# Blocks 0 and 1 of the first layer take turns, and eight attention steps form the start

## The chip, the cores and the metric

The kernel runs on one core of a Trainium2 chip. The engines that matter are TensorE (PE in the profile; its weight loads are PEld), VectorE (DVE), ScalarE (ACT), GpSimd (POOL), and SyncE (SP), which here issues DMAs. The metric is the device time of one execution in microseconds; less is better.

## What is computed

Attention over chunks of 32 queries with 8 memory keys, then two dense layers, each up, activation, down. Cut to what matters:

```
q, k, v: (4, 8, 768, 64)    mem_k, mem_v: (4, 8, 8, 64)
for each chunk c of 32 queries:
    k_full = concat(mem_k, k[c*32-16 : c*32+40]);  v_full likewise
    a = softmax(q_c @ k_full.T / 8);               out_c = a @ v_full
x = out as 3072 tokens x 512
h = x @ w_in1;  x = (h * sigmoid(1.702 * h)) @ w_out1     # 512 -> 2048 -> 512
h = x @ w_in2;  x = (max(h,0) + alpha * min(h,0)) @ w_out2
```

## The kernel before

**Tiling.** The 3072 tokens are cut into six blocks of 512, the 2048 hidden units into 16 chunks of 128. A *step* is one block and one chunk f: `mm1` makes the hidden tile h (12 matmuls of 128x512, L312), the activation and `split_g` make from it a high part gh and a low part gl (ACT and DVE), and `mm2_t` adds the chunk's share to four PSUM banks y0 to y3 (12 matmuls, L342). Every product is made of three matmuls, high x high, high x low and low x high, so a step has 24. Layer 1 has 96 steps, layer 2 another 96. mm2 trails mm1 by one step (`LAG`). After a block's last chunk `finish1` scales the four banks and stores them to the DRAM tensor y1, from which layer 2 reads.

**Weights.** Chunk f of a layer is loaded by `w_load` (two DMAs of 512 KB, L85 and L89), then prepared by `w_abs` (ACT, L96), `w_bits` (four DVE instructions on 128x1024, L102 to L109), `w_high` (ACT, L120) and `w_low` (DVE, L125). `w_tick` does one such chunk and loads ahead. Layer 1 prepares its 16 chunks while block 0 runs through all of them; later blocks find them ready in SBUF.

**Attention.** 24 *attention steps* of 128 tokens give the input x of the blocks, four steps to a block. A step loads q, k and v (512, 416 and 416 KB), makes scores (32 small PE instructions in the profile, L195), maximum, difference and exponential (DVE, DVE, ACT), sum and scaling (DVE, L227 to L232), transposes in two groups (PE, L242), copies them (ACT, L247), multiplies with v (L256), and writes the high part of x by ACT (L270) and the low part by DVE (L271). An mm1 of a block reads all 512 tokens, so it needs all four steps.

**Order.** Steps 0 to 3 run ahead of the main loop (L425 on) in a pool with two places for loads (`SB = 2`). Then the main loop goes through the steps, block by block, and `attend` spreads the later attention steps evenly: steps 4 to 7 during block 0, and so on. A scheduler turns this into one fixed order for each engine. Each engine and each DMA queue works through its own order; an instruction whose input is missing holds all behind it. All loads and stores stand in SP's queue.

Of the kernel before, what the change touches and what calls it, by code (L numbers as in the profile page):

```python
# [31 lines left out]
P2_BLOCKS = [512] * 6  # L32
TBM = 512
LAG = 1
NSTART = 4
WTICKS = (2, 3)
WAHEAD = 2
LEAD = 4
OPB = 3
W0 = 3  # L40
WN = 5
# [8 lines left out]
def fused_kernel(ctx: ExitStack, tc: tile.TileContext, qs, ks, vs, ident, w_in1, w_out1, w_in2, w_out2, alpha, out):  # L50
    nc = tc.nc
    PSUM = bass.MemoryType.PSUM
    const = ctx.enter_context(tc.tile_pool(name="const", bufs=1))
# [76 lines left out]
    def w_tick(limit):  # L130
        s = wtick[0]
        if s >= limit + 1:
            return False
        if s - 1 in wst:
            w_low(s - 1)
        while wloaded[0] < limit and wloaded[0] <= s + (WAHEAD if wloaded[0] < BOOST else 1):
# [20 lines left out]
    run = [slice(0, KW), slice(NK - KW, NK)]  # L157
    half = [slice(0, 64), slice(64, 128)]

    def att_open(name, bufs, nq):  # L160
        ap["pb"] = 2 * bufs if bufs > 1 else 1
# [13 lines left out]
        return (ps2 if tag == "h" else ps1).tile(shape, F32, tag=tag, name=name)  # L175

    def a_load(m):
        q = ap["pool"].tile([128, 2, HP, 2, 64], F32, tag="q", name=f"q{m}")
        nc.sync.dma_start(out=q.rearrange("p g j c q -> p (g j c q)"), in_=qs[m])
        k = ap["pool"].tile([128, 2, HP, NK], F32, tag="k", name=f"k{m}")  # L180
        nc.sync.dma_start(out=k.rearrange("p g j n -> p (g j n)"), in_=ks[m])
        st[m] = dict(q=q, k=k)

    def a_load_v(m):
        t = ap["pool"].tile([NK, 2, VC], F32, tag="v", name=f"v{m}")
        nc.sync.dma_start(out=t, in_=vs[m])
        st[m]["v"] = t

# [34 lines left out]
    def a_norm(m):  # L223
        s = st[m]
        ex = s["ex"]
        sm = ap["pool"].tile([128, 2 * HP], F32, tag="sm", name=f"sm{m}")
        nc.vector.tensor_reduce(out=sm, in_=ex, axis=mybir.AxisListType.X, op=ALU.add)  # L227
        nc.vector.tensor_scalar(out=sm, in0=sm, scalar1=1e-9, scalar2=None, op0=ALU.add)
        nc.vector.reciprocal(sm, sm)
        pr = ap["pr"][m % len(ap["pr"])]  # L230
        for c in range(2):
            nc.vector.tensor_tensor(  # L232
                out=pr[half[c], :, :, run[c]].rearrange("p g j n -> p (g j) n"), in0=ex[half[c]],
                in1=sm[half[c]].rearrange("p (g n) -> p g n", n=1).to_broadcast([64, 2 * HP, KW]), op=ALU.mult,
            )
        s["pr"] = pr

    def a_trans(m, g, tag=None):
        s = st[m]
        s["pt", g] = bank([NK, HP, 128], tag or f"a{g}", f"pt{m}_{g}")  # L240
        for j in range(HP):
            nc.tensor.transpose(s["pt", g][:, j, :], s["pr"][:, g, j, :], id_sb)  # L242

    def a_pcopy(m, g):
        s = st[m]
        s["p", g] = ap["pool"].tile([NK, HP, 128], F32, tag=f"p{g}", name=f"p{m}_{g}", bufs=ap["pb"] if g == 0 else None)
        nc.scalar.copy(s["p", g], s["pt", g])  # L247

    def a_pv(m, tag="a0"):
# [87 lines left out]
    def mm2_t(p, y, gs, n, f):  # L337
        gh, gl = gs
        wh, wl = wt[p, f]
        for m in range(NKC):  # L340
            for i, (w, g) in enumerate(((wh, gh), (wh, gl), (wl, gh))):
                nc.tensor.matmul(  # L342
                    y[m][:, :n], w[:, 1, m * 128:(m + 1) * 128], g[:, :n],
                    start=(f == 0 and i == 0), stop=(f == NF - 1 and i == 2),
                )

    def mm2_n(p, y, gs, n, f):
# [6 lines left out]
                    start=(f == 0 and i == 0), stop=(f == NF - 1 and i == 2),  # L354
                )

    def finish1(y, t0, n):
        for m in range(NKC):
            o = op.tile([128, TBM], F32, tag="o", name="o")
            if m % 2:  # L360
# [30 lines left out]
    steps = []  # L391
    t0 = 0
    for j, n in enumerate(P1_BLOCKS):
        steps += [(1, j, t0, n, f) for f in range(NF)]
        t0 += n
    t0 = 0
    for j, n in enumerate(P2_BLOCKS):
        steps += [(2, j, t0, n, f) for f in range(NF)]
        t0 += n
    n1 = len(P1_BLOCKS)  # L400
    need = [done_tick(int(p1_start[j + 1]) // SQ - 1) for j in range(n1)]
    last1 = (n1 - 1) * NF

    pend = {}
    ys = {}
# [5 lines left out]
    for i in range(NWARM):  # L411
        nc.tensor.matmul(t, warm, warm, start=True, stop=True)

    att_open("as", SB, 2)
    a_load(0)
    a_load_v(0)
    w_load(0)
    nc.sync.dma_start(out=id_sb, in_=ident)
    a_load(1)
    wloaded[0] = 1  # L420
    stags = ("a0", "a1", "y2", "y3")
# [3 lines left out]
    for t in range(NSTART + 1):  # L425
        if t + 1 < NSTART:
            a_scores(t + 1, stags[(t + 1) % 4])
            a_load_v(t + 1)
        if t + 2 < NSTART:
            a_load(t + 2)  # L430
        if t < NSTART:
            a_norm(t)
            for g in range(2):
                a_trans(t, g, "h")
                a_pcopy(t, g)
        if t + 1 < NSTART:
# [12 lines left out]
    att_open("at", 1, 1)
    a_load(NSTART)  # L450
    a_load_v(NSTART)

    def do_mm2(i):
        p, j, t0, n, f = steps[i]
        if f == 0:
            ys[p, j] = [ps1.tile([128, DM], F32, tag=f"y{m}", name=f"y{m}") for m in range(NKC if p == 1 else n // 128)]
        (mm2_t if p == 1 else mm2_n)(p, ys[p, j], pend.pop(i), n, f)
        if f == NF - 1:
            (finish1 if p == 1 else finish2)(ys.pop((p, j)), t0, n)

    def attend(j, h):
        goal = need[j] + (need[j + 1] - need[j]) * min(1, h / (2 * NF - LEAD))
        while tick[0] < goal:
            a_tick()

    for i, (p, j, t0, n, f) in enumerate(steps):
        if i < NF:
            while wtick[0] < min(NPC + 1, W0 + (WN * f) // 4):
                w_tick(NPC)
        if i == last1:  # L470
# [71 lines left out]
```

## Time and profile before

| | us |
|---|---|
| median of 3 runs (1182.45 to 1184.22) | 1183.54 |
| the profiled execution | 1184.33 |
| its span, first to last instruction | 1182.6 |
| PE busy, share of span | 1150.4, 97% |
| DVE busy | 611.1, 52% |
| ACT busy | 321.5, 27% |

[...] The timeline lists instructions with the idle time before each and what ended it, in brackets. Matmuls overlap in the records (one of 128x512 lasts 0.39 us, the next starts 0.23 us later), so that their pace is read from runs of many, not from one.

### The profile page before, as it was taken

The numbers are of one execution on the slowest core, as the hardware profiler recorded it, in microseconds if no ns is written. First come the engines' busy times: TensorE is split into PE (matmuls) and PEld (weight loads), VectorE is DVE, ScalarE is ACT, GpSimd is POOL, SyncE is SP. The second block draws the span as 40 slices with busy tenths as digits, with TensorE's granted clock in tenths as the row PEclk, the third lists the DMA queues.
The fourth block names the chain that finished last, engine by engine and source line by source line (L and its number), as shares of the span: only waits on it lengthen the run. The fifth ranks groups of instructions, "written<-read, shape, count | busy, mean of one in ns | idle before, by whom it ended". The sixth has DMA issues, their size and how long they took to land.

```text
span 1182.6 us, 14925 instructions
## 1 busy us (share of the span) xinstructions
PE 1150.4 (97%) x6364; PEld 942.3 (80%) x6364; DVE 611.1 (52%) x871; ACT 321.5 (27%) x479; POOL 2.4 (0%) x10
## 2 busy tenths in 40 slices
PE   5799999999999999999999999999999999999998
PEld 5577788888888888888888788888888888888886
DVE  5899934343343434343699874434434434344433
ACT  2555433232323223223456321111111111111111
POOL 0000000000000000000000000000000000000000
PEclk8799999999999999999999999999999999999999
DMA  6964313121121212112544500200100000000000
GB/s 211 275 220 155 133 69 94 47 75 55 50 91 60 70 48 83 48 62 71 191 166 145 189 23 1 72 1 5 67 1 1 36 1 1 36 1 8 29 1 36
DMA packets 43578, 86.49 MB, mean 73 GB/s; under 512 B 5048, under 2 KB 21560, under 8 KB 43512
## 3 DMA queue, kind: packets, MB, share of 16 engines
q1 hardware_dynamic: 43512, 85.54, 21.9%
q8 instruction: 50, 0.82, 0.3%
q14 instruction: 16, 0.13, 0.0%
HBM read 72.95 MB, written 12.58 MB: 72 GB/s over the span
## 4 chain that ended last, share of the span: by engine, by line
PE 90%; DVE 4%; DMA 4%; ACT 1%; issue 1%; SPq 0%; ACTq 0%
PE h L312 42%; PE y L352 21%; PE y L342 21%; DMA wraw<-w_out 2%; PE xp L256 2%; PE sc L195 2%; PE pt L242 2%; DMA k<-ks 1%; DVE wtmp L109 1%; DVE wtmp L106 1%; DVE wlo L125 1%; DVE wtmp L102 0%; ACT wtmp L96 0%; DVE gl L334 0%; DVE atpr L232 0%
## 5 line engine op out<-in xcount | busy, mean ns | idle before, releaser
L312 PE MATMUL h<-x,whi 128*128 128x512 f32 x768 | 244.6, 398 | 2.7 <-ACT whi L120 1.9
L312 PE MATMUL h<-yx,whi 128*128 128x512 f32 x768 | 239.1, 390 | 1.1 <-DVE t L327 1.1
L333 ACT CAST gh<-t 128x512 fp32r<-128x512 f32 x192 | 119.2, 621 | 441.2 <-DVE t L327 372.5
L334 DVE TENSOR_TENSOR gl<-t,gh 128x512 fp32r<-128x512 f32 x192 | 132.4, 690 | 106.7 <-ACT gh L333 106.3
L326 DVE TENSOR_SCALAR t<-h,al_sb 128x512 f32<-128x512 f32 x96 | 72.0, 750 | 196.1 <-PE h L312 196.1
L312 PEld LDWEIGHTS h<-x,whi 128*128 128x128 f32 x768 | 143.8, 190 | 34.3 <-ACT whi L120 3.5
L312 PEld LDWEIGHTS h<-yx,whi 128*128 128x128 f32 x768 | 144.1, 188 | 32.4 <-DVE t L327 1.6
L321 DVE SCALAR_TENSOR_TENSOR t<-t,h 128x512 f32<-128x512 f32 x96 | 65.8, 685 | 184.9 <-ACT t L320 184.5
L312 PE MATMUL h<-x,wlo 128*128 128x512 f32 x384 | 152.1, 396 | 0.5 <-DVE wlo L125 0.5
L342 PE MATMUL y<-gl,whi 128*128 128x512 f32 x384 | 151.3, 394 | 0.4 <-DVE gl L334 0.4
L342 PE MATMUL y<-gh,wlo 128*128 128x512 f32 x384 | 150.7, 392 | 0.0
L312 PE MATMUL h<-yx,wlo 128*128 128x512 f32 x384 | 149.9, 390 | 0.0
L352 PE MATMUL y<-whi,gh 128*128 128x512 f32 x384 | 149.8, 390 | 0.0
L352 PE MATMUL y<-wlo,gh 128*128 128x512 f32 x384 | 149.7, 390 | 0.0
L352 PE MATMUL y<-whi,gl 128*128 128x512 f32 x384 | 142.6, 390 | 0.0
L342 PE MATMUL y<-gh,whi 128*128 128x512 f32 x384 | 128.1, 398 | 3.4 <-ACT gh L333 3.2
L320 ACT ACTIVATE t<-h 128x512 f32<-128x512 f32 x96 | 57.4, 598 | 185.5 <-PE h L312 185.4
L342 PEld LDWEIGHTS y<-gh,whi 128*128 128x128 f32 x384 | 70.7, 188 | 20.5 <-ACT gh L333 5.5
L312 PEld LDWEIGHTS h<-x,wlo 128*128 128x128 f32 x384 | 72.6, 189 | 16.7 <-DVE wlo L125 0.9
L342 PEld LDWEIGHTS y<-gl,whi 128*128 128x128 f32 x384 | 72.6, 189 | 16.3 <-DVE gl L334 0.8
L342 PEld LDWEIGHTS y<-gh,wlo 128*128 128x128 f32 x384 | 72.5, 189 | 15.6
L312 PEld LDWEIGHTS h<-yx,wlo 128*128 128x128 f32 x384 | 72.1, 188 | 15.5
(50 smaller groups left out, 916.0 us busy)
## 6 DMA issues: line engine op xcount, KB each, us to landing
wraw<-w_in SPq DMA_DIRECT2D x32, 512.0 KB
wraw<-w_out SPq DMA_DIRECT2D x32, 512.0 KB
q<-qs SPq DMA_DIRECT2D x24, 512.0 KB
k<-ks SPq DMA_DIRECT2D x24, 416.0 KB
v<-vs SPq DMA_DIRECT2D x24, 416.0 KB
y<-o SPq DMA_DIRECT2D x24, 256.0 KB
yraw<-y SPq DMA_DIRECT2D x6, 1024.0 KB
out<-o SPq DMA_DIRECT2D x24, 256.0 KB
```

Source lines behind the costliest of these rows:

```text
L106: nc.vector.scalar_tensor_tensor(out=a, in0=top, scalar=0xC0000000, in1=a, op0=ALU.bitwise_and, op1=ALU.bitwise_or)
L195: nc.tensor.matmul(sc[half[c], g, j, :], s["q"][:, g, j, c], s["k"][:, g, j, run[c]], start=True, stop=True,)
L242: nc.tensor.transpose(s["pt", g][:, j, :], s["pr"][:, g, j, :], id_sb)
L256: nc.tensor.matmul(x[half[z], g, j, :].rearrange("p (c q) -> p c q", c=2), s["v"][:, g, (2 * j + z) * D:(2 * j + z + 1) * D], p[:, j, z], ...
L312: nc.tensor.matmul(h[:, :n], w[:, 0, k * 128:(k + 1) * 128], x[:, z, k, :n], start=(i == 0), stop=(i == 3 * NKC - 1))
L320: nc.scalar.activation(out=t[:, :n], in_=h[:, :n], func=AF.Tanh, scale=1.702 / 2)
L321: nc.vector.scalar_tensor_tensor(out=t[:, :n], in0=t[:, :n], scalar=1.0, in1=h[:, :n], op0=ALU.add, op1=ALU.mult)
L326: nc.vector.tensor_scalar(out=t[:, :n], in0=h[:, :n], scalar1=0.0, scalar2=al_sb[:, f:f + 1], op0=ALU.min, op1=ALU.mult)
L333: nc.scalar.copy(gh[:, :n], g[:, :n])
L334: lo_eng.tensor_tensor(out=gl[:, :n], in0=g[:, :n], in1=gh[:, :n].bitcast(F32), op=ALU.subtract)
L342: nc.tensor.matmul(y[m][:, :n], w[:, 1, m * 128:(m + 1) * 128], g[:, :n], start=(f == 0 and i == 0), stop=(f == NF - 1 and i == 2),)
L352: nc.tensor.matmul(y[m], g[:, m * 128:(m + 1) * 128], w[:, 1, :], start=(f == 0 and i == 0), stop=(f == NF - 1 and i == 2),)
```

## The change

The order of the first layer's blocks 0 and 1 is cut into four phases: block 0 with chunks 0 to 5, block 1 with chunks 0 to 5, block 0 with chunks 6 to 15, block 1 with chunks 6 to 15. After a first part `finish1` scales the banks on ACT and stores them to y1 by DMAs from ACT's own queue; near the end of the second part `load_part` reads them back, and DVE adds them as it scales. Attention steps 4 to 7, block 1's input, move into the first four steps of the main loop; steps 8 to 11 fall into the fourth phase, 10 steps long.

The start has five places for the loads of k and q and six for v, three for the exponentials; its scores go through the banks a0, y2, y3 and a0, and from step 4 on have bank a1 for themselves, while transposes and products use a0. The q of the first eight attention steps is loaded without its zeros (two DMAs of 128 KB) into tiles that POOL fills with zeros, and PE reads it with a stride. The first eight chunks get their low part at once.

```diff
-NSTART = 4
-WTICKS = (2, 3)
+NFIRST = 4
+NSTART = 8
+HEAD = 6
+WTICKS = (1, 3)
-SB = 2
-NWB = 4
+SB = 5
+NWB = 8
...
+            if s < HEAD + 2:
+                w_low(s)
...
     def a_load(m):
+        if m < NSTART:
+            q = ap["pool"].tile([128, 2, 2, CHUNK, 2 * HP], F32, tag="q", name=f"q{m}")
+            for z in range(2):
+                nc.gpsimd.memset(q[half[z], :, 1 - z], 0.0)
+                nc.sync.dma_start(out=q[half[z], :, z].rearrange("p g q i -> p g (q i)"), in_=q0[m, half[z]])
+            q = q.rearrange("p g z q (j c) -> p g j c (z q)", j=HP)
...
+    def load_part(j):
+        t0, n = int(p1_start[j]), P1_BLOCKS[j]
+        t = wr.tile([128, NKC, TBM], F32, tag="wraw", name=f"part{j}", bufs=2)
+        nc.sync.dma_start(out=t[:, :, :n], in_=y1[:, :, t0:t0 + n].rearrange("k p t -> p k t"))
+        parts[j] = t
+
+    def finish1(y, j, last):
+        t0, n = int(p1_start[j]), P1_BLOCKS[j]
+        if not last:
+            for m in range(NKC):
+                o = op.tile([128, TBM], F32, tag="o", name="o")
+                nc.scalar.mul(o[:, :n], y[m][:, :n], 0.5)
+                nc.scalar.dma_start(out=y1[m, :, t0:t0 + n], in_=o[:, :n])
+            return
...
+    phases = [(0, 0, HEAD), (1, 0, HEAD), (0, HEAD, NF), (1, HEAD, NF)]
+    phases += [(j, 0, NF) for j in range(2, len(P1_BLOCKS))]
...
+        now = NFIRST + i if i < NSTART - NFIRST else None
+        if now is not None:
+            a_norm(now)
+            if now + 1 < NSTART:
+                a_scores(now + 1, "a1")
+                a_max(now + 1)
+                a_exp(now + 1)
+            for q in range(2):
+                a_trans(now, q, "a0")
+                a_pcopy(now, q)
+            a_pv(now, "a0")
+            a_xcopy(now)
```

What the scheduler makes of it is seen in three places. The first is SP's queue during the start (q, k, v are an attention step's loads, wraw_2 the load of weight chunk 2; the last number only counts buffers). Before, from the loads of attention steps 2 and 3 on:

```order
L179 DMA q_186<-qs 128x1024
L181 DMA k_188<-ks 128x832
L179 DMA q_254<-qs 128x1024
L181 DMA k_256<-ks 128x832
L186 DMA v_252<-vs 104x1024
L186 DMA v_320<-vs 104x1024
L85 DMA wraw_1_366<-w_in 128x4x256
L89 DMA wraw_1_366<-w_out 128x1024
L85 DMA wraw_2_369<-w_in 128x4x256
L89 DMA wraw_2_369<-w_out 128x1024
L85 DMA wraw_3_421<-w_in 128x4x256
```

Of the change, from the load of alpha on (the loads of steps 0 to 5 and of chunks 0 and 1 stand ahead):

```order
L481 DMA al_sb<-alpha 128x16x1
L184 DMA q_409<-q 64x2x256 x2
L187 DMA k_414<-ks 128x832
L198 DMA v_416<-vs 104x1024
L85 DMA wraw_2_457<-w_in 128x4x256
L89 DMA wraw_2_457<-w_out 128x1024
L184 DMA q_470<-q 64x2x256 x2
L187 DMA k_475<-ks 128x832
L198 DMA v_477<-vs 104x1024
L85 DMA wraw_3_564<-w_in 128x4x256
L89 DMA wraw_3_564<-w_out 128x1024
```

Chunk 2 now stands behind the loads of steps 0 to 6, chunk 3 behind those of steps 0 to 7; before, chunks 1 to 3 stood behind those of steps 0 to 3 alone.

The second place is ACT's queue at the end of the start (p is a step's transposed probabilities, x_232 and x_255 block 0's input, wtmp<-wraw the first operation on a weight chunk). Before:

```order
L96 ACTIVATE wtmp<-wraw_1_366 128x1024
L247 COPY p_0_392<-pt_0_387 104x512
L247 COPY p_1_399<-pt_1_394 104x512
L96 ACTIVATE wtmp<-wraw_2_369 128x1024
L270 CAST x_232<-xp_401 128x2x4x64
L120 CAST whi_1_430<-wtmp 128x1024
```

Of the change:

```order
L96 ACTIVATE wtmp<-wraw_2_457 128x1024
L282 CAST x_255<-xp_390 128x2x4x64
L259 COPY p_0_429<-pt_0_424 104x512
L259 COPY p_1_436<-pt_1_431 104x512
L233 ACTIVATE ex_497<-ex_497 128x512
L96 ACTIVATE wtmp<-wraw_3_564 128x1024
L282 CAST x_255<-xp_438 128x2x4x64
L120 CAST whi_2_576<-wtmp 128x1024
```

The last write of block 0's input (x_255<-xp_438) stood behind the load of chunk 2 and stands now behind that of chunk 3.

The third place is the passage from block 0 to block 1, which before had other matmuls of block 0 beside it. PE before (x_232 is block 0's input, x_672 block 1's):

```order
L312 MATMUL h_1397<-x_232,wlo_15_1211 128x512
L312 MATMUL h_1429<-x_672,whi_0_378 128x512 x2
L312 MATMUL h_1429<-x_672,wlo_0_379 128x512
L312 MATMUL h_1429<-x_672,whi_0_378 128x512 x2
L312 MATMUL h_1429<-x_672,wlo_0_379 128x512
L312 MATMUL h_1429<-x_672,whi_0_378 128x512 x2
L312 MATMUL h_1429<-x_672,wlo_0_379 128x512
L312 MATMUL h_1429<-x_672,whi_0_378 128x512 x2
L342 MATMUL y_565<-gh,whi_14_1115 128x512
```

PE of the change (x_561 is block 1's input, pt and xp attention step 7):

```order
L354 MATMUL y_698<-gl,whi_5_865 128x512
L354 MATMUL y_698<-gh,wlo_5_866 128x512
L254 MATMUL pt_0_823<-id_sb,aspr_125 104x128 x4
L254 MATMUL pt_1_830<-id_sb,aspr_125 104x128 x4
L268 MATMUL xp_837<-p_0_828,v_477 64x64 x8
L268 MATMUL xp_837<-p_1_835,v_477 64x64 x8
L324 MATMUL h_1017<-x_561,whi_0_334 128x512
L324 MATMUL h_1061<-x_561,whi_1_466 128x512
```

ACT of the change at the same passage (o<-y is `finish1`'s scaling, y_83<-o its store):

```order
L382 ACTIVATE o<-y_695 128x512
L382 ACTIVATE o<-y_696 128x512
L383 DMA y_83<-o 128x512 x2
L382 ACTIVATE o<-y_697 128x512
L259 COPY p_0_828<-pt_0_823 104x512
L383 DMA y_83<-o 128x512
L259 COPY p_1_835<-pt_1_830 104x512
L382 ACTIVATE o<-y_698 128x512
L383 DMA y_83<-o 128x512
L282 CAST x_561<-xp_837 128x2x4x64
L120 CAST whi_6_924<-wtmp 128x1024
```

Block 0's chunk is finished, step 7's last stage and the stores stand between it and block 1's first matmul; before, that matmul stood in front of 24 matmuls that block 0 still had.

## Rows read from the trace of the kernel before

**Rows 1.** The page: busy tenths and granted clock in 40 slices.
```profile
DVE  5899934343343434343699874434434434344433
PEclk8799999999999999999999999999999999999999
```
**Rows 2.** Windows: length, busy us (count) by engine, clock, DMA share, GB/s.
```profile
44.00:152.78 108.78, 103.79 (x679) 81.63 (x680) 102.72 (x141) 55.40 (x74) 0.00 (x0) 0.96 0.56 184
```
**Rows 3.** The same stretch, PE and PEld of L312, L342, L195, L242, L256.
```profile
44.00:152.78 108.78, 51.86 (x191) 37.08 (x192) 0.96 0.56 184
44.00:152.78 108.78, 44.02 (x168) 31.81 (x168) 0.96 0.56 184
44.00:152.78 108.78, 5.65 (x160) 5.17 (x160) 0.96 0.56 184
44.00:152.78 108.78, 4.14 (x32) 3.64 (x32) 0.96 0.56 184
44.00:152.78 108.78, 5.29 (x128) 4.32 (x128) 0.96 0.56 184
```
**Rows 4.** Chain that ended last, in order of time: start us, us, what.
```profile
44.00 5.91 PE h L312 x13
...
56.29 2.72 PE y L342 x12
...
133.25 3.81 PE y L342 x12
```
**Rows 5.** Timeline of PE: start us, us, instruction, [idle before <-releaser].
```profile
44.00 1.22 PE L312 MATMUL h<-x,whi 128*128 128x512 f32 x2 [1.67 <-ACT whi L120]
...
130.59 1.21 PE L342 MATMUL y<-gh,whi 128*128 128x512 f32 x4 [2.08 <-ACT gh L333]
...
152.78 0.62 PE L312 MATMUL h<-x,whi 128*128 128x512 f32 x2
```
**Rows 6.** Timeline of SP: DMA issues of the start, and stores.
```profile
7.98 6.94 SPq L179 DMA_DIRECT2D q<-qs  x1
...
17.42 12.73 SPq L186 DMA_DIRECT2D v<-vs  x2
30.20 0.40 SPq L85 DMA_DIRECT2D wraw<-w_in  x1
...
160.94 3.09 SPq L364 DMA_DIRECT2D y<-o  x4
```
**Rows 7.** Windows for the DMA rate, its last two columns.
```profile
3.00:14.00 11.00, 4.20 (x48) 3.78 (x47) 5.02 (x10) 1.75 (x2) 0.12 (x1) 1.00 1.01 329
14.00:16.00 2.00, 2.00 (x29) 1.63 (x29) 1.93 (x3) 1.17 (x2) 0.00 (x0) 1.00 0.80 32
16.00:24.00 8.00, 3.35 (x80) 3.06 (x77) 5.66 (x10) 2.06 (x3) 0.00 (x0) 0.71 0.82 288
58.00:64.00 6.00, 6.00 (x28) 4.99 (x27) 6.00 (x11) 2.35 (x4) 0.00 (x0) 1.00 1.05 383
```
**Rows 8.** Timeline of ACT.
```profile
39.87 1.15 ACT L96 ACTIVATE wtmp<-wraw 128x1024 f32<-128x1024 f32 x1 [0.69 <-DMA wraw<-w_out]
...
69.01 1.07 ACT L247 COPY p<-pt 104x512 f32<-104x512 f32 x2 [3.15 <-PE pt L242]
...
128.91 1.12 ACT L96 ACTIVATE wtmp<-wraw 128x1024 f32<-128x1024 f32 x1 [2.27 <-DMA wraw<-w_out]
...
163.08 0.60 ACT L361 ACTIVATE o<-y 128x512 f32<-128x512 f32 x1 [0.32 <-DMA y<-o]
```
**Rows 9.** Timeline of DVE, four in a row, then a pair.
```profile
103.86 1.21 DVE L106 SCALAR_TENSOR_TENSOR wtmp<-wraw,wtmp 128x1024 uint32<-128x1024 uint32 x1
105.00 0.67 DVE L321 SCALAR_TENSOR_TENSOR t<-t,h 128x512 f32<-128x512 f32 x1
105.59 0.68 DVE L214 TENSOR_TENSOR ex<-sc,mx 128x512 f32<-128x512 f32 x1
106.19 0.68 DVE L102 TENSOR_SCALAR wtmp<-wtmp 128x1024 f32<-128x1024 f32 x1
...
116.28 1.38 DVE L232 TENSOR_TENSOR atpr<-ex,sm 64x512 f32<-64x512 f32 x2
```

More of the change, by code (lines that the diff above doesn't have):

```diff
@@ L135, in w_tick @@
             w_low(s - 1)
-        while wloaded[0] < limit and wloaded[0] <= s + (WAHEAD if wloaded[0] < BOOST else 1):
+        while wloaded[0] < limit and wloaded[0] <= s + (1 if s < 2 else WAHEAD if wloaded[0] < BOOST else 1):
             w_load(wloaded[0])
@@ L184, in a_load_v @@
     def a_load_v(m):
-        t = ap["pool"].tile([NK, 2, VC], F32, tag="v", name=f"v{m}")
+        t = ap["pool"].tile([NK, 2, VC], F32, tag="v", name=f"v{m}", bufs=SB + 1 if m < NSTART else 1)
         nc.sync.dma_start(out=t, in_=vs[m])
@@ L245, in a_pcopy @@
         s = st[m]
-        s["p", g] = ap["pool"].tile([NK, HP, 128], F32, tag=f"p{g}", name=f"p{m}_{g}", bufs=ap["pb"] if g == 0 else None)
+        s["p", g] = ap["pool"].tile([NK, HP, 128], F32, tag=f"p{g}", name=f"p{m}_{g}", bufs=ap["pb"] if g == 0 else (ap["pb"] + 1) // 2)
         nc.scalar.copy(s["p", g], s["pt", g])
@@ L343, in mm2_t @@
                     y[m][:, :n], w[:, 1, m * 128:(m + 1) * 128], g[:, :n],
-                    start=(f == 0 and i == 0), stop=(f == NF - 1 and i == 2),
+                    start=(f == fa and i == 0), stop=(f == fb - 1 and i == 2),
                 )
@@ L355, in mm2_n @@
                 )
-    def finish1(y, t0, n):
+    parts = {}
+    def load_part(j):
[10 more added lines that the diff above has]
+                nc.scalar.dma_start(out=y1[m, :, t0:t0 + n], in_=o[:, :n])
+            return
+        part = parts.pop(j, None)
         for m in range(NKC):
             o = op.tile([128, TBM], F32, tag="o", name="o")
-            if m % 2:
+            if part is not None:
+                nc.vector.scalar_tensor_tensor(
+                    out=o[:, :n], in0=y[m][:, :n], scalar=0.5, in1=part[:, m, :n], op0=ALU.mult, op1=ALU.add
+                )
+            elif m % 2:
                 nc.scalar.mul(o[:, :n], y[m][:, :n], 0.5)
@@ L389, in split_y @@
         xt[100 + j] = x
[L391 to L395, printed above, removed]
+    phases = [(0, 0, HEAD), (1, 0, HEAD), (0, HEAD, NF), (1, HEAD, NF)]
+    phases += [(j, 0, NF) for j in range(2, len(P1_BLOCKS))]
+    steps = [(1, ph, j, int(p1_start[j]), P1_BLOCKS[j], f) for ph, (j, a, b) in enumerate(phases) for f in range(a, b)]
     t0 = 0
     for j, n in enumerate(P2_BLOCKS):
-        steps += [(2, j, t0, n, f) for f in range(NF)]
+        steps += [(2, None, j, t0, n, f) for f in range(NF)]
         t0 += n
-    n1 = len(P1_BLOCKS)
-    need = [done_tick(int(p1_start[j + 1]) // SQ - 1) for j in range(n1)]
-    last1 = (n1 - 1) * NF
+    n1 = len(phases)
+    need, top = [], 0
+    for j, _, _ in phases:
+        top = max(top, j)
+        need.append(done_tick(int(p1_start[top + 1]) // SQ - 1))
+    last1 = sum(b - a for _, a, b in phases[:-1])
     pend = {}
@@ L412, in fused_kernel @@
         nc.tensor.matmul(t, warm, warm, start=True, stop=True)
-    att_open("as", SB, 2)
+    att_open("as", SB, 2, 3)
     a_load(0)
     a_load_v(0)
+    nc.sync.dma_start(out=id_sb, in_=ident)
     w_load(0)
[L418 to L421, printed above, removed]
+    for m in range(1, NFIRST):
+        a_load(m)
+        a_load_v(m)
+        if m == 2:
+            w_load(1)
+    wloaded[0] = 2
+    stags = ("a0", "y2", "y3", "a0")
     a_scores(0, stags[0])
@@ L424, in fused_kernel @@
     a_exp(0)
[L425 to L436, printed above, removed]
+    for t in range(NFIRST):
+        if t + 1 < NFIRST:
+            a_scores(t + 1, stags[t + 1])
+        a_norm(t)
+        for g in range(2):
+            a_trans(t, g, "h")
+            a_pcopy(t, g)
+        if t + 1 < NFIRST:
@@ L450, in fused_kernel, with steady @@
-    a_load(NSTART)
-    a_load_v(NSTART)
-    def do_mm2(i):
-        p, j, t0, n, f = steps[i]
+    a_scores(NFIRST, "a1")
+    a_max(NFIRST)
+    a_exp(NFIRST)
+    def steady():
+        att.close()
+        side["wpb"] = ctx.enter_context(tc.tile_pool(name="wpb", bufs=NWB))
+        att_open("at", 1, 1, 1)
+    def do_mm2(i):
+        p, ph, j, t0, n, f = steps[i]
+        if p == 1:
+            _, fa, fb = phases[ph]
+            if f == fa:
+                ys[ph] = [ps1.tile([128, TBM], F32, tag=f"y{m}", name=f"y{m}") for m in range(NKC)]
+            mm2_t(p, ys[ph], pend.pop(i), n, f, fa, fb)
+            if f == fb - 1:
+                finish1(ys.pop(ph), j, fb == NF)
+            return
@@ L455, in do_mm2 @@
         if f == 0:
-            ys[p, j] = [ps1.tile([128, DM], F32, tag=f"y{m}", name=f"y{m}") for m in range(NKC if p == 1 else n // 128)]
-        (mm2_t if p == 1 else mm2_n)(p, ys[p, j], pend.pop(i), n, f)
+            ys[p, j] = [ps1.tile([128, DM], F32, tag=f"y{m}", name=f"y{m}") for m in range(n // 128)]
+        mm2_n(p, ys[p, j], pend.pop(i), n, f)
         if f == NF - 1:
-            (finish1 if p == 1 else finish2)(ys.pop((p, j)), t0, n)
-    def attend(j, h):
-        goal = need[j] + (need[j + 1] - need[j]) * min(1, h / (2 * NF - LEAD))
+            finish2(ys.pop((p, j)), t0, n)
@@ L463, in attend @@
+    def attend(ph, f, half_step):
+        _, a, b = phases[ph]
+        span = 2 * (b - a) - (LEAD if b - a > HEAD else 1)
+        goal = need[ph] + (need[ph + 1] - need[ph]) * min(1, (2 * (f - a) + half_step) / span)
         while tick[0] < goal:
             a_tick()
-    for i, (p, j, t0, n, f) in enumerate(steps):
-        if i < NF:
-            while wtick[0] < min(NPC + 1, W0 + (WN * f) // 4):
+    for i, (p, ph, j, t0, n, f) in enumerate(steps):
+        if NSTART - NFIRST <= i < last1:
+            while wtick[0] < min(NPC + 1, 3 + i if i < HEAD else 3 + HEAD + (3 * (i - HEAD)) // 4):
@@ L469, in fused_kernel @@
                 w_tick(NPC)
+        now = NFIRST + i if i < NSTART - NFIRST else None
[10 more added lines that the diff above has]
+            a_xcopy(now)
+            while wtick[0] < min(3 + i, NF - 2 - NWB):
+                w_tick(NPC)
+            if now + 1 == NSTART:
+                steady()
@@ L470, in fused_kernel @@
+        if p == 1 and f == NF - 2 and ph == 2:
+            a_load(NSTART)
+            a_load_v(NSTART)
         if i == last1:
@@ L483, in fused_kernel @@
         if i < last1:
-            attend(j, 2 * f + 2)
+            attend(ph, f, 2)
+        if p == 1 and f == NF - 2 and phases[ph][1] > 0:
+            load_part(j)
         q = i - last1 - LAG
@@ L503, in _layout @@
     G = GPB
+    q0 = q.reshape(B, HP, 2, G, 2, CHUNK, D).transpose(0, 3, 2, 6, 5, 1, 4).reshape(NSG, 2, 128, HP * QG).transpose(0, 2, 1, 3)
     qs = np.zeros((B, G, 2, D, HP, 2, 2, CHUNK), np.float32)
```

35 lines of the change are left out of this document (17 added, 18 removed).

## The prediction

> **What bounds the kernel now.** I read the 40 slices first [rows 1]. TensorE is busy nearly throughout, but the fifth to eighth slices show DVE full as well, after a start in which the clock was below its upper level. So the first 150 us have another limit than the rest. From there on PE alone sets the time, and the change leaves PE's matmuls as they are, so that it can win only what PE loses before block 1 is under way.
>
> That loss is read from the stretch between block 0's first full matmuls and block 1's first one, 44.00 to 152.78 [rows 2, 5]. It holds 191 matmuls of L312 and 168 of L342 [rows 3]. At the upper clock twelve take 2.72 us [rows 4], 0.2267 each, so the 359 need 81.4. The attention matmuls add 5.65 + 4.14 + 5.29 = 15.1 [rows 3]. Together 96.5 of 108.78 us: **12.3 us are lost.** Of these 5.0 are idle (108.78 less 103.79 busy [rows 2]). [...] DVE is busy for 102.7 of the stretch [rows 2]: it prepares 16 weight chunks while block 0 already wants them.
>
> The start before 44 is bound by loads. SP stood 6.94 and 12.73 us before it could pass step 2's and step 3's loads, and only at 30.20 came chunk 1's [rows 6].
>
> **The change part by part.** *Start.* With five and six places SP no longer waits for PE's reading, so the DMAs run through from about 3 us. The bytes ahead of a landing then decide. An attention step brings 0.262 (q without zeros) + 0.426 + 0.426 = 1.11 MB, a chunk 1.05 MB. Up to chunk 2 the new queue has 7 steps, 3 chunks and the identity, 11.0 MB; up to chunk 3, 13.2 MB. The mixed early loads moved 329 GB/s, weights alone 383 [rows 7]. Alpha's load costs 2 us in which next to nothing else moves, 32 GB/s [rows 7]. So chunk 2 lands at 3 + 2 + (28.7 to 33.5), 34 to 38.5, chunk 3 at 39.5 to 45. I take 37 and 43, nearer to the mixed row, since eight attention steps are among them.
>
> [...]
>
> ACT and DVE take chunk 2 ahead of the end of step 3 (the order above). ACT's operation takes 1.1 [rows 8]; DVE then has two wide operations of 1.14, eight of 0.60, a pair of 1.4 and small ones of 0.5 until block 0's last low part [paces from rows 9], 9.0 in all. That is 37 + 1.1 + 9.0 = **47.1** for block 0's first full matmul, 3.1 later than now. Chunk 3, at 43, delays nothing more unless it lands after 45. Bounds 44 to 49. When block 0 starts, two score groups (1.13 each) and one transpose (1.03) of later steps are behind PE [rows 3], 3.3 to the good.
>
> [...]
>
> *First phase.* DVE's queue from 47.1 until block 1's input is complete: 14 wide operations (16.0), 33 of 0.60 (19.8), three pairs (4.1), small ones 1.3 [rows 9], together 41 us. PE's: 6 steps x 24 x 0.2267 = 32.6, scores, transposes and products up to step 6 8.4 [rows 3], clock 3.0, together 44. So PE covers DVE, by 3 us, where before DVE was the later one. If that cover is gone, each us shows on PE. [...]
>
> *Passage from block 0 to block 1.* PE has nothing but step 7 between block 0's chunk 5 and block 1. ACT's queue there: two scalings are done when PE ends, then two store issues (0.33 to 0.5 each, nearest SP's [rows 6]), a scaling 0.6, a copy 0.54, an issue, a copy, the fourth scaling, an issue, the high part of x 0.6 [rows 8]; DVE's low part 0.6 follows. That is 5.4 us, in which PE has 1.03 + 1.32 us of work [rows 3]. **3.0 us idle.** The fourth scaling also needs the first store landed; the like wait cost 0.32 [rows 8] and is covered by the copies. Bounds 1 and 6, since no store issued by ACT is in the trace. Behind it the clock may fall as it did after 2.08 idle us: 1.1 [rows 4, 5], bounds 0 and 3. Then four wide ACT operations for chunks 6 to 9 (4.4) stand before block 1's first activation. PE fills both h banks and 13 scores, 6.4 us; the first bank is free after 4.4 + 0.6 + 2.8 on DVE. **1.4 us idle.**
>
> *With one answer.* From chunk 6 on weights have three steps for every four and phases three and four want none new before their turn: hidden. The two extra sets of scalings, the reload and DVE's addition (same instruction count as the scaling) lie beside 16 steps of PE work. Passages 2 and 3 have a whole h tile ahead of the first y, over 3 us, against 2.4 for four scalings: covered. Steps 8 to 11 come twice as fast, one in 10.9 us, with 4.5 us of DVE work each and no weights: covered, up to 2 us if not. POOL's zeros come before the loads land. PE's strided reading of q isn't in the trace; its weight loads run beside matmuls (81.6 of 108.8 [rows 2]), so 0, and up to a doubled score group, 1.1 each for steps 6 and 7.
>
> **Sum.** 12.3 - 3.1 + 3.3 - 3.0 - 1.0 - 3.0 - 1.1 - 1.4 = 3.0 us less. The profiled execution took 1184.33, its span of 1182.6 and 1.7 around it; that gives 1181.3. It stands 0.79 above the median of the runs, so I forecast a median of **1180.5**.
>
> **The rivals.** *Early start, 0.17.* All loads run at 383, chunk 2 lands at 34 and block 0 starts at 44; the denser small matmuls have lifted the clock by then. 3.1 + 3.0 more, and 1.1 if it stays up: 10.2 us less, 1173.3. For it: the DMA share was 1.0 wherever loads were queued [rows 7]. Against it: 329 with attention loads in them.
>
> *DVE still late, 0.18.* Two queues with a margin of 3 us in 44 wait for each other in turn, and DVE's last items end block 1's input, not PE. 2.5 us lost more, 1183.0. For it: DVE was full to 95% and PE lost in gaps even so [rows 2]. Against: the row sums.
>
> *Late chunk 3, slower, 0.20.* ACT's first operation on chunk 3 stands ahead of the last high part of block 0's input, so that one load holds block 0. This is seen now: at 128.91 ACT had waited 2.27 for a load, the gh behind it was late, and PE stood 2.08 [rows 5, 8]. If the early loads run at the 288 of the stretch at 16 to 24, chunk 3 lands at 3 + 2 + 45.8 = 50.8 and block 0 starts near 53, 6 us after my forecast: 1186.5. It decides from a start at 50 on, where the sum is zero. Against it: that stretch had 2 us without anything queued.
>
> **How the numbers follow.** About 0.2%, 2.4 us, is what a measurement of this kernel can tell. The forecast has 0.45. Of it 0.37 lie over 2.4 us below 1183.5 and 0.08 within; its own range is 1177 to 1184. With the early start faster has 0.54, the late DVE and the forecast's rest make 0.26 within 0.2%, slower has 0.20. The range reaches from the early start, 1173, to just past the late chunk, 1187.
>
> **What would show it.** In the changed profile: SP without waits of over 5 us before 30; ACT's first operation on chunk 2 at about 38 and on chunk 3 at 44; block 0's run of L324 starting at 46 to 48, its first ten matmuls at 0.45 each; an idle PE of about 3 us before block 1's first h, some 90 to 97 us after the start, behind ACT's write of x; no idle PE of 2 us behind a weight load up to 150; and from block 1's second part on the paces of before. It would be wrong if chunk 3 lands after 46, if the passage costs more than 6, or if the later phases show waits for ACT's stores.

## The result, and the profile after

The change made the kernel slower: a median of 1199.97 us against 1183.82 on the same chip, ratio 1.0138 (95% interval 1.0109 to 1.0167). The profiled execution took 1201.54, its span is 1199.7, 17.1 longer than before.

The page gives DVE's busy share and TensorE's granted clock in tenths, here in 40 slices of 30.0 us. The slices that answer to [rows 1] show DVE lower in the second slice (6, before 8) and the clock lower in the second and third (6 and 8, before 7 and 9):

```profile
DVE  4697962544434343433499883533434434434443
PEclk9689999999999999999999999999999999999999
```

The loss lies ahead of block 0. The timeline of PE, where [rows 5] stood (start, length, instruction, idle time before it):

```profile
53.42 1.12 PE L268 MATMUL xp<-p,v 104*64 104x64 f32 x16 [7.82 <-ACT p L259]
...
60.28 1.22 PE L324 MATMUL h<-x,whi 128*128 128x512 f32 x2 [2.17 <-ACT x L282]
...
71.54 2.11 PE L207 MATMUL sc<-k,q 128*64 128x64 f32 x32
...
112.57 1.22 PE L324 MATMUL h<-x,whi 128*128 128x512 f32 x3 [0.69 <-ACT x L282]
...
120.36 0.74 PE L324 MATMUL h<-x,whi 128*128 128x512 f32 x2 [0.82 <-DVE t L333]
```

Block 0's matmuls begin at 60.28 instead of 44.00, 16.3 us later, and that is nearly all of the 17.1. (Before, a single one stood ahead of that run, at 41.53.)

```profile
41.53 0.79 PE L312 MATMUL h<-x,whi 128*128 128x512 f32 x1 [0.82 <-ACT x L270]
```

The chain that ended last, cut to this start, says through what (start, length, what):

```profile
10.42 10.90 DMA k<-ks
21.32 0.02 issue
21.34 11.29 DMA q<-q
...
33.13 7.38 SPq L184
...
41.89 5.04 DMA v<-vs
46.93 0.02 issue
46.95 11.60 DMA wraw<-w_out
...
58.63 1.13 ACT wtmp L96
59.76 0.48 ACT x L282
...
60.28 1.22 PE h L324 x2
```

Loads, one behind the other, and SP's stand behind alpha fill the time; then ACT works on chunk 3 (L96 at 58.63) and only behind it on the high part of x that block 0 waits for. The loads are slow, not few. The windows that answer to [rows 7] (busy by engine, then clock, DMA share, GB/s):

```profile
3.00:14.00 11.00, 3.38 (x43) 2.95 (x41) 4.07 (x9) 1.75 (x2) 6.31 (x13) 1.00 1.03 274
16.00:24.00 8.00, 6.08 (x97) 5.77 (x99) 4.78 (x6) 2.55 (x4) 1.04 (x2) 1.00 1.06 254
24.00:39.00 15.00, 8.53 (x119) 7.71 (x114) 11.08 (x18) 4.80 (x7) 1.04 (x2) 0.68 0.95 217
```

The DMA engines were busy throughout (share 0.95 to 1.06) and moved 274, 254 and 217 GB/s (the last with alpha's small packets in it), where before they moved 329 at such a share. ACT shows when the chunks came (as in [rows 8]):

```profile
51.28 1.12 ACT L96 ACTIVATE wtmp<-wraw 128x1024 f32<-128x1024 f32 x1 [9.00 <-DMA wraw<-w_out]
...
58.63 1.13 ACT L96 ACTIVATE wtmp<-wraw 128x1024 f32<-128x1024 f32 x1 [2.98 <-DMA wraw<-w_out]
```

Chunk 2 is taken at 51.28, forecast for 37, and chunk 3 at 58.63, forecast for 43.

### The profile page after: what moved, and what is told of

It is laid out like the page before. It is cut to its first block, busy times and chain, and to the rows that moved or that the text cites. A ratio compares the mean times of both kernels' runs of the same rounds, so it can differ in the third digit from the quotient of the medians.

```text
span 1199.7 us, 14981 instructions
## 1 busy us (share of the span) xinstructions
PE 1155.3 (96%) x6364; PEld 947.4 (79%) x6364; DVE 613.3 (51%) x875; ACT 321.5 (27%) x483; POOL 10.7 (1%) x26
## 4 chain that ended last, share of the span: by engine, by line
PE 91%; DMA 5%; DVE 2%; SPq 1%; ACT 1%; issue 0%; ACTq 0%; DVEq 0%
PE h L324 43%; PE y L354 22%; PE y L364 21%; PE xp L268 2%; PE pt L254 2%; PE sc L207 2%; DMA wraw<-w_out 1%; DMA q<-q 1%; DMA k<-ks 1%; SPq L184 1%; DMA y<-o 1%; DMA wraw<-w_in 1%; DMA v<-vs 0%; DVE wtmp L106 0%; ACT wtmp L96 0%
## 5 line engine op out<-in xcount | busy, mean ns | idle before, releaser
L332 ACT ACTIVATE t<-h 128x512 f32<-128x512 f32 x96 | 57.3, 597 | 195.2 <-PE h L324 195.1
L364 PEld LDWEIGHTS y<-whi,gh 128*128 128x128 f32 x384 | 72.1, 188 | 15.4
L364 PEld LDWEIGHTS y<-wlo,gh 128*128 128x128 f32 x384 | 72.1, 188 | 15.3
```

The lines of the kernel that those rows point to most:

```text
L332: nc.scalar.activation(out=t[:, :n], in_=h[:, :n], func=AF.Tanh, scale=1.702 / 2)
L364: nc.tensor.matmul(y[m], g[:, m * 128:(m + 1) * 128], w[:, 1, :], start=(f == 0 and i == 0), stop=(f == NF - 1 and i == 2),)
```

## The experiments

Times are set against the kernel before on the same chip, as a ratio with its 95% interval. Beside the time I use one number worked out from the PE timeline, the *loss behind the start*: from block 0's first large matmul to the start of PE's last matmul, less 0.2267 us for each of the 4608 large ones and 0.0333, 0.0985 and 0.0345 for each one of scores, transposes and products (their pace in undisturbed runs). It is 31.2 before and 31.6 after; counted from the run at 44.00 it is 29.0 before. Each such number comes from the one profiled execution of its kernel.

**The form of the q loads.** q of steps 0 to 7 is loaded whole:

```diff
-            for z in range(2):
-                nc.gpsimd.memset(q[half[z], :, 1 - z], 0.0)
-                nc.sync.dma_start(out=q[half[z], :, z]..., in_=q0[m, half[z]])
+        nc.sync.dma_start(out=q..., in_=qs[m])
```

> The changed kernel, but q of steps 0 to 7 is loaded as before the change, in one load of 512 KB with its zeros; no halves, no zeroing by GpSimd. In the changed kernel chunk 2's first operation came at 51.28 and block 0 at 60.28, since the early loads moved some 230 GB/s instead of the 329 to 383 of the prediction. Theory one, the form of the q loads (two loads over 64 partitions each, runs of 1 KB) holds the DMAs up: up to chunk 2 there are now 12.8 MB instead of 11.0, and at 330 GB/s that is 39 us, so chunk 2 at about 44, block 0 at about 53, time 1192. Theory two, the rate doesn't depend on q's form (it is v's form, or attention loads as such): 12.8 MB at 230 take 56, so chunk 2 at 61, block 0 at 70, time 1208. In both, a score group behind block 0's start takes 1.13 us again instead of 2.1, if q's strided reading is what made it 2.1.

1186.8, ratio 1.0034 (1.0018 to 1.0050): theory one, and more than it expected. Block 0 starts at 48.6, though 1.8 MB more are loaded ahead of chunk 2. A score group behind the start takes 1.15 again. The loss behind the start is 28.5, 3.1 less than in the changed kernel, of which the two score groups make 2.2.

```profile
57.41 1.15 PE L197 MATMUL sc<-k,q 128*64 128x64 f32 x32
```

**The form of the v loads.** 24 rows of zeros are added to v's layout:

```diff
-        t = ap["pool"].tile([NK, 2, VC], F32, tag="v", ...)
+        t = ap["pool"].tile([128, 2, VC], F32, tag="v", ...)
```

> The changed kernel, but v is laid out over 128 partitions (24 rows of zeros that no matmul reads), so that its load goes over 128 partitions instead of 104: 512 KB instead of 416. Theory one, v's form over 104 partitions holds the early loads up: up to chunk 2 there are 11.7 MB instead of 11.0, at 330 GB/s 35 us, so chunk 2 at about 40, block 0 at about 50, time 1190. Theory two, q's halves do: the rate stays at 230, chunk 2 at 54, block 0 at 63, time 1203.

1195.5, ratio 1.0108 (1.0086 to 1.0129), block 0 at 53.3. The time is 0.3% below that of the changed kernel instead of the 0.8% of theory one, and the two intervals overlap. The start came 7.0 us earlier, with a loss behind it of 33.9. So v's form seems to have a part (the next run but one shows it more plainly), and q's has the larger one.

**Alpha later.** The load's line is moved 14 steps down in the code.

> The changed kernel, but alpha (2048 packets of 4 bytes) is loaded 14 steps into the work on the blocks instead of between the loads of steps 5 and 6. In the changed kernel SP stood 7.38 us behind it and from 39 to 42 the DMAs moved 59 GB/s. If alpha costs what those 3 us show, all that stands behind it comes 2.4 us earlier: block 0 at 58, time 1197.5. If SP's 7.38 us count, block 0 comes at 53, time 1193. If the rate of the loads behind it sets the end anyway, nothing: 1200.

1203.9, ratio 1.0174 (1.0153 to 1.0195). It didn't test what it was meant to: nothing binds this load, the scheduler issued it at 41.25, and SP stood 7.03 behind it as before. Block 0 started at 58.9.

**The three together.**

> The three edits together: q whole, v over 128 partitions, alpha late. Up to chunk 2 there are 13.5 MB. If the form of the loads was the cause, they now move at the 380 GB/s of whole loads: 35.5 us from 3 on, chunk 2 at 39, chunk 3 at 45, block 0 at 48 to 50, time 1184 to 1187. If attention loads are slow whatever their form, 13.5 MB at 230 to 260 take 52 to 59, block 0 at 64 or later, time 1203 or more.

1181.68, ratio 0.9990 (0.9981 to 0.9999), block 0 at 43.3. Alpha was again issued early, at its old place between the loads of steps 5 and 6, with SP standing 6.93, so that this run differs from the one with whole q by v's form alone. The form of the loads was the cause: no other edit is needed to take back the 16 us.

One thing changed along with it. In this kernel, as in those with only q whole or only v over 128 partitions, the scheduler puts the last high part of block 0's input ahead of ACT's first operation on chunk 3, so that block 0 no longer waits for chunk 3. ACT in this run (the second L96 is chunk 3's):

```profile
41.65 1.12 ACT L96 ACTIVATE wtmp<-wraw 128x1024 f32<-128x1024 f32 x1 [2.48 <-DMA wraw<-w_out]
42.67 0.56 ACT L272 CAST x<-xp 128x512 fp32r<-128x512 f32 x1
...
48.79 1.14 ACT L96 ACTIVATE wtmp<-wraw 128x1024 f32<-128x1024 f32 x1
```

In the changed kernel the products that this input is made of were done at 57.3, ACT wrote it at 59.65, and PE stood 2.17 ahead of 60.28. So some 2 of the 16 us belong to ACT's order. Chunk 2 is taken 9.6 us earlier here.

**Alpha in another layout**, transposed on the host, so that the load has 128 packets of 64 bytes instead of 2048 of 4. First with whole q and v over 128 partitions, then alone in the changed kernel:

```diff
-nc.sync.dma_start(out=al_sb, in_=alpha.rearrange("(f p) -> p f", p=128))
+nc.sync.dma_start(out=al_sb, in_=alpha)
```

> The changed kernel with q whole, v over 128 partitions and alpha as 128 packets of 64 bytes. With alpha as 2048 packets of 4 bytes SP stood 6.93 us in the earlier run of q and v, and the DMAs moved 54 GB/s from 30 to 33. If alpha's packets cost that, chunk 2's last load lands at 37.5 instead of 41.56, block 0 starts at 40 instead of 43.3, time 1178.5. If by then step 3's softmax sets the start, block 0 starts at 42.5 and the time is 1181.

> The changed kernel with alpha alone in the form of 128 packets of 64 bytes. The run with alpha's issue moved didn't settle its price: the load is bound to nothing, so that it went out at 41.25 instead of 32.65 and SP stood 7.03 behind it all the same. If SP's standing costs the DMAs 3 us with nothing queued, block 0 starts at 57 and the time is 1196.5; if the slow forms of q and v set the end whatever SP does, 1200.

The first: 1180.18, ratio 0.9984 (0.9975 to 0.9992). SP's stand is gone, chunk 2 is taken at 39.8 instead of 41.7, and block 0 starts at 43.44 all the same: the second theory. The chain of this kernel, ahead of the start:

```profile
35.64 0.68 DVE aspr L234
36.34 0.70 DVE aspr L234
37.17 1.08 PE pt L244 x4
38.37 0.44 issue
38.81 0.64 ACT ex L223
39.48 0.70 DVE sm L229
40.64 0.68 DVE aspr L234
41.34 0.69 DVE aspr L234
42.06 0.70 DVE wtmp L102
```

With fast loads the chain runs through DVE. The second: 1200.29, ratio 1.0155 (1.0130 to 1.0181), no gain in the medians, as its second theory has it. But in its profiled execution (1198.51) block 0 starts 2.6 us earlier, as the first theory has it:

```profile
57.69 1.22 PE L324 MATMUL h<-x,whi 128*128 128x512 f32 x2 [2.21 <-ACT x L282]
```

Its four runs lie between 1197.34 and 1205.90, so whether SP's stand, 7.38 us of the chain above, costs nothing or some 3 us they can't tell. It isn't the cause of the 16 us.

**Why the forms are slow.** v over 112 partitions instead of 128, the rest as in the last but one:

```diff
-        t = ap["pool"].tile([128, 2, VC], F32, tag="v", ...)
+        t = ap["pool"].tile([112, 2, VC], F32, tag="v", ...)
```

> The changed kernel with the three fast forms, but v over 112 partitions instead of 128. If it matters that 104 rows divide badly (104 = 13 x 8, 112 = 16 x 7), v's loads are fast again: k's packets stay at 135 ns, block 0 starts at 43.5, time 1180. If it matters that a load covers other partitions with its parts than those of 128 do, k's packets go back to about 200 ns in the stretch from 3 to 40, block 0 starts at 47 to 49, time 1184 to 1187. [...]

1186.62, ratio 1.0021 (1.0011 to 1.0030), block 0 at 47.4: slow like 104 (1.0034, 48.6), as the second theory has it, though k's packets took 144 ns (below), not its 200. So how the rows divide is not what makes them slow.

Then q in two halves of 64 rows again, but on even and odd partitions, so that each spans all 128:

```diff
-                nc.gpsimd.memset(q[half[z], :, 1 - z], 0.0)
-                nc.sync.dma_start(out=q[half[z], :, z]..., in_=q0[m, half[z]])
+                nc.sync.dma_start(out=q[z:128:2, :, z]..., in_=q0[m, half[z]])
```

> Loads of q in halves as in the changed kernel, but the two halves lie on even and odd partitions (2d and 2d + 1 for row d of either half, in q and k alike) instead of 0 to 63 and 64 to 127, so that each load spans all 128; GpSimd zeroes the whole tile first. v over 128 partitions and alpha in 128 packets, so that it is to be set against the run with v alone over 128 partitions (1195.5; 305 GB/s from 16 to 24; block 0 at 53.3) and the one with q whole as well (1180.2; 396; 43.4). If the halves are slow because each reaches only one half of the partitions, the rate from 16 to 24 goes to 380 or more, and the time to 1182 to 1184 (PE's strided reading of q, some 2 us, stays). If a load of 64 rows is dealt out to the DMA engines otherwise than one of 128, and this is what slows the rest, the rate stays near 300 and the time near 1195. [...]

The rate went up, the time did not. From 16 to 24 us, for v alone over 128 partitions, q whole as well, v over 112, and q on even and odd partitions (one row of the windows from each kernel):

```profile
16.00:24.00 8.00, 6.51 (x96) 5.88 (x93) 6.20 (x9) 2.65 (x4) 2.07 (x4) 0.68 1.06 305
```
```profile
16.00:24.00 8.00, 3.60 (x82) 3.38 (x79) 6.94 (x12) 3.65 (x5) 0.00 (x0) 0.94 1.04 396
```
```profile
16.00:24.00 8.00, 3.76 (x86) 3.43 (x82) 7.02 (x12) 3.62 (x5) 0.00 (x0) 0.99 1.05 345
```
```profile
16.00:24.00 8.00, 3.09 (x36) 2.93 (x37) 7.82 (x13) 2.80 (x3) 0.95 (x1) 1.00 1.04 390
```

305, 396, 345 and 390 GB/s. So a half of q is slow since it reaches only partitions 0 to 63 or 64 to 127, not since it is small or has 64 rows. (On even and odd partitions it isn't quite as fast as whole: 352 and 372 GB/s from 3 to 14 and 24 to 36 us, where whole q moved 382 and 400.) The trace holds each packet's size and time; their means, of those that began from 3 to 36 us:

```
mean ns of one packet      3328 B (k)  4096 B (v, w_out, q whole)  1024 B (w_in, q halves)
before                        137         207                         63
after                         217         243                         71
q whole, v over 104           141         207                         60
q halves, v over 128          208         199                         63
q whole, v over 112           144         204                         57
q whole, v over 128           135         164                         52
q even and odd, v over 128    142         169                         49
```

The halves of q hold up the other loads too: k's own form never changed, and its packets took 208 to 217 ns with halves of q beside them, instead of 135. With v over 104 or 112 and q whole they took 141 and 144. The time stayed at 1194.7, ratio 1.0103 (1.0086 to 1.0120), for other reasons: the whole tile is zeroed ahead of the loads, step 0's q lands late and the first scores come 5 us later. The first scores, at 5.98 in the changed kernel:

```profile
10.65 4.13 PE L207 MATMUL sc<-k,q 128*64 128x64 f32 x64 [6.49 <-DMA q<-q]
```

Block 0 starts at 48.7, 5.3 us later than with whole q, and the loss behind it is 35.5, 6.2 more. Of these some 2.4 are two score groups at the slow pace, and 2.2 longer waits in the passage from block 0 to block 1 (5.2 us idle instead of 3.0); why these are longer stays open.

**Turns alone.** With fast loads, blocks 0 and 1 one after the other:

```diff
-    phases = [(0, 0, HEAD), (1, 0, HEAD), (0, HEAD, NF), (1, HEAD, NF)]
-    phases += [(j, 0, NF) for j in range(2, len(P1_BLOCKS))]
+    phases = [(j, 0, NF) for j in range(len(P1_BLOCKS))]
```

The weight chunks go back to five for every four steps with it.

> The changed kernel without its turns: block 0 runs all 16 chunks, then block 1, as before the change; weight chunks at five for every four steps again. Loads in the fast form: q whole, v over 128 partitions, alpha as 128 packets of 64 bytes (its layout transposed on the host). To be set against the same kernel with turns. If the turns save what the prediction put on them (of the 12.3 us lost before, 2.8 net of the passages), this one is 3 us slower than with turns. If what they save on DVE goes into the passages, the two are within 1 us. Before the change PE lost 29.0 us after block 0's start, and in the changed kernel with fast loads of q and v also 29.0, which speaks for the second.

1181.37, ratio 0.9987 (0.9977 to 0.9997), against 0.9984 with turns: 0.4 us by the ratios, 1.2 by the medians, and the intervals overlap. The loss behind the start is 31.1 without and 29.3 with turns, so they do save 1.8, but without them block 0 starts 1.4 earlier, at 42.1.

**Fast loads in the kernel before:** v over 128 partitions and alpha in 128 packets, nothing else.

> The kernel before the change, with v over 128 partitions and alpha as 128 packets of 64 bytes, nothing else. Before, SP stood 6.94 us behind alpha ahead of step 2's q, and 12.73 ahead of step 3's v for a place. If alpha's standing and v's form hold the start, block 0 starts 3 to 6 us before 44.0, time 1177 to 1180. If the places hold it (SP waits for PE's reading of steps 0 and 1), it starts at 43 to 44 and the time stays within 1.5 us of 1182.7.

1179.47, ratio 0.9968 (0.9956 to 0.9980): the lowest ratio of all kernels here, though its interval overlaps with others. So with fast loads on both sides the change as a whole (0.9984) gains nothing. What v's form and what alpha's give here, the run doesn't tell apart. Its SP stands 8.57 where [rows 6] shows 12.73:

```profile
17.59 8.57 SPq L186 DMA_DIRECT2D v<-vs  x2
```

Block 0's run starts at 40.08, 3.9 earlier than before, and the loss from there is 28.9 (29.0 before, counted alike).

**Weights ahead of attention steps.** As with fast loads, and

```diff
+    w_load(2)
+    w_load(3)
-    wloaded[0] = 2
+    wloaded[0] = 4
```

> The changed kernel with the three fast forms (q whole, v over 128 partitions, alpha in 128 packets), and chunks 2 and 3 loaded ahead of the attention steps 4 to 7 instead of between steps 6 and 7 and behind them. There, block 0 started at 43.44 and the time was 1180.2. Ahead of chunk 3's end there are now 10.4 MB, at 400 GB/s 26 us, so it lands at about 30. If the loads set the start, block 0 starts at about 38, of which the score groups of steps 4 and 5, now behind the start, take 2.2 back: 1177. If DVE does (busy for 13.8 of the 15 us from 15 to 30, and 12.6 of the next), it starts at 42 to 43 and the time stays at 1180 to 1182.

1186.18, ratio 1.0023 (1.0014 to 1.0032), which neither theory had: block 0 starts at 49.0. DVE is full, and two chunks now stand in its order ahead of the softmax that block 0 needs. Its window from 30 to 45, and the transposes that wait:

```profile
30.00:45.00 15.00, 7.04 (x79) 6.32 (x78) 14.96 (x21) 5.80 (x8) 0.00 (x0) 0.50 1.04 400
```
```profile
43.53 1.92 PE L244 MATMUL pt<-id_sb,aspr 128*104 128x128 f32 x8 [7.49 <-DVE aspr L234]
```

The loss behind the start falls to 26.9, which fits that more weights are ready by then: early work and late work of DVE change places.

**The passage from block 0 to block 1.** With fast loads, two of four scalings on DVE, the stores on SP, the last transposes in bank a1; then the same with the stores on ACT:

```diff
-                nc.scalar.mul(o[:, :n], y[m][:, :n], 0.5)
-                nc.scalar.dma_start(out=y1[m, :, t0:t0 + n], in_=o[:, :n])
+                if m % 2:
+                    nc.scalar.mul(o[:, :n], y[m][:, :n], 0.5)
+                else:
+                    nc.vector.tensor_scalar(out=o[:, :n], in0=y[m][:, :n], scalar1=0.5, ...)
+                nc.sync.dma_start(out=y1[m, :, t0:t0 + n], in_=o[:, :n])
```

> The changed kernel with the three fast forms, and a lighter passage from block 0 to block 1: two of the four scalings of the partial sum on DVE, the stores issued by SP, and the second transposes of step 7 in the bank a1. In the run with the fast forms alone PE stood 0.79, 0.84, 0.68 and 0.68 us there and its matmuls behind it ran at half pace from 92.1 to 98.2 (some 2.9 us lost). If ACT's scalings and the shared bank make the waits, 1.5 to 2 us of idle go: 1178.5, and 1175.5 if the half pace goes as well. If the chain of step 7 (softmax, copies, product, x) sets it, the time stays at 1180.

> As the run with the lighter passage, but the stores of the partial sum are issued by ACT as in the changed kernel (two of the four scalings still on DVE, the second transposes of step 7 in bank a1). With the stores on SP, PE's idle time in the passage fell from 3.0 to 1.7 us and its clock stayed at the upper level, but step 8's k, queued on SP behind the stores and a weight chunk, came 4.15 us late at 100.45, and the time stayed at 0.9985 of before. If that wait was all that took the gain, it is gone now (without the stores on SP, k's issue stood at 91.9 instead of 93.0 and no chunk ahead of it): 1177 to 1178. If the k wait comes back since block 1 starts earlier than step 8 can be loaded, 1180 to 1181.

1181.66, ratio 0.9985 (0.9976 to 0.9994), then 1180.50, 0.9977 (0.9966 to 0.9987). In both the passage is shorter and the clock behind it stays up (granted 1.00 from 92 to 100 us, 0.62 with fast loads alone; two large matmuls in a row last 0.62 us there instead of 1.05), and in both step 8's k is then what comes late, first by 3.99 and, with SP free of the stores, by 2.51:

```profile
90.48 1.22 PE L314 MATMUL h<-x,whi 128*128 128x512 f32 x3 [0.69 <-ACT x L272]
...
100.45 1.59 PE L197 MATMUL sc<-k,q 128*64 128x64 f32 x32 [3.99 <-DMA k<-ks]
```
```profile
99.22 1.15 PE L197 MATMUL sc<-k,q 128*64 128x64 f32 x32 [2.51 <-DMA k<-ks]
```

The intervals of the two and of the kernel with fast loads alone overlap: with this wait in it, the lighter passage gains nothing that these runs can tell (0.8 us by the best ratio).

## Why the prediction was wrong

**The step that failed is the load rate.** It put chunk 2 at 37 and chunk 3 at 43, with 13.2 MB at 329 to 383 GB/s [rows 7]. The rows of before hold no load like the halves of q, and the prediction counted them by their bytes. Measured are 274, 254 and 217 GB/s, chunk 2 at 51.28, chunk 3 at 58.63. Block 0's start, forecast at 47.1, came at 60.28: 13.2 of the 20.1 us between forecast (3.0 less) and result (17.1 more). Another 5.4 are loss behind the start (31.6, where the sum makes 29.0 less 2.8), and 1.0 attention not done ahead. With whole q and v over 128 partitions block 0 starts at 43.3, even before the forecast.

The runs show that it matters which partitions a half covers: with v over 128 partitions, 305 GB/s from 16 to 24 us with halves of q in one half each, and 390 with even and odd ones, which span all 128.

**v's form** has no term in the sum. It costs: 1.0034 with v over 104 against 0.9990 over 128 is 0.44%, 5.2 us (alpha's load stands at the same place in both queues). 112 rows gave 1.0021, slow as well. The mixed loads at 329 GB/s in [rows 7] had v over 104 partitions among them, and the prediction didn't ask whether it was v that slowed them. With whole q the same window moves 337 with v over 104 partitions and 384 with v over 128:

```profile
3.00:14.00 11.00, 4.41 (x49) 3.98 (x48) 5.24 (x10) 1.92 (x3) 0.11 (x1) 1.00 1.02 337
```
```profile
3.00:14.00 11.00, 4.69 (x51) 4.24 (x49) 5.48 (x11) 2.20 (x3) 0.11 (x1) 1.00 1.02 384
```

**The rival with chunk 3** had the place and the sign: ACT's first operation on chunk 3 stands ahead of the high part of x at 59.65, and block 0 starts behind it. It was priced with 288 GB/s, start 53, 1186.5; the rate was lower still. The forecast's own path, from chunk 2 through 9.0 us of DVE, was not the one taken: the chain runs from chunk 3 through ACT.

**Attention ahead.** Two score groups are done, no transposes: 2.3 us instead of 3.3.

**PE's strided reading of q**, taken as 0 with a bound of 1.1 for each of two groups, was at its bound: 2.11 and 2.38 instead of 1.13 [rows 3], and 1.15 with whole q, which is read without the stride. Why the strided reading takes about twice as long, the runs don't show.

**The clock and the gaps.** The first 3.0 that the sum takes off is the clock at block 0's start. Before, the 13 matmuls there took 5.91 us [rows 4] where 13 x 0.2267 make 2.95, and the granted clock was 0.53 from 44.00 to 50.40. The changed kernel had 0.50 from 60.28 to 66.70: 3.2 us lost, an estimate from half a clock for 6.42 us. The 1.0 behind it stands for gaps in the first phase, and no run shows it; the runs show the loss behind the start as a whole, 31.2 before and 31.6 after.

**The passage** came as forecast or better: 0.84, 0.68 and 0.69 idle (2.2 for 3.0), no fall of the clock (0 for 1.1), and 0.82 for the h banks (1.4). In the kernel with fast loads the clock did fall there (0.62 from 92 to 100 us), behind 3.0 us idle.

**Hidden steps.** DVE's addition of the partial sum was put down as covered. It stood 3.48 for a store that held its place, and step 11's scaling, queued behind it, held PE for 1.69 (DVE, then PE):

```profile
281.09 0.69 DVE L389 SCALAR_TENSOR_TENSOR o<-y,part 128x512 f32<-128x512 f32 x1 [3.48 <-DMA y<-o]
281.70 1.38 DVE L244 TENSOR_TENSOR atpr<-ex,sm 64x512 f32<-64x512 f32 x2
```
```profile
283.22 1.05 PE L254 MATMUL pt<-id_sb,atpr 128*104 128x128 f32 x8 [1.69 <-DVE atpr L244]
```

By the paces above, the changed kernel loses 8.4 us from 152.78 to 300, where the kernel before loses 3.9. This wait makes 1.9 of it, and passing between attention matmuls and large ones 3.5 instead of 1.6; the prediction put these phases at nothing, or at 2 us if steps 8 to 11 were not covered.

**What the turns save** was oversized too. Forecast were 12.3 us of loss turned into 9.5. With fast loads the loss behind the start is 29.3, 1.9 us less than before (31.2) and 1.8 less than without turns. It may be that DVE has the same work either way, so that an earlier block 0 leaves more of it behind the start (31.1 from 42.1, 29.3 from 43.4, 26.9 from 49.0), but this isn't shown: with v over 112 it is 30.2 from 47.4.

**A slip in reading.** The prediction has DVE full in the fifth to eighth slices. In [rows 1] it is the third to fifth, 59 to 148 us; the conclusion, that the first 150 us have another limit, stands.

## What to carry to other kernels

Price a load by the partitions that it covers, not by its bytes: leaving out zeros saved 0.26 MB a step and made k's packets beside it 54% slower (217 ns against 141), and padding v with zeros made the kernel with whole q 0.44% faster. Where a DMA share of 1.0 comes with different rates in the same trace (329 and 383 GB/s in [rows 7]), find out which load is in the slow stretches before a rate is carried over to a new mix. Before hiding or moving a start, add up the work of the engine that fills it: with DVE full, loads that came sooner moved its work about, and gained 1 to 4 us of the 12 that PE lost.

## What the runs showed of the hardware

With only loads over all 128 partitions in flight, the core's DMAs moved 396 to 401 GB/s (16 to 24 and 15 to 30 us of the kernel with fast loads), more than the 383 of weights alone [rows 7]. Loads over 64 partitions in one half slow down the packets of others: k's by 54% (from 135 to 208 ns with v over 128 partitions, from 141 to 217 with v over 104). With loads over 104 or 112 partitions the rate falls too (345 GB/s from 16 to 24 us in both, instead of 396), but k's packets hardly change (141 and 144 ns). Why 112 and 104 are slow stays open: they miss only the last partitions, and the runs don't tell whether the way their rows are dealt out or those missing partitions matter.
